# One level of Strassen's algorithm in the last big product of a three-stage kernel

## The chip, the cores and the metric

The kernel runs on one core of a Trainium2 chip. Its metric is device time in microseconds (us), from the program's start to its end, and the time given is the median of three runs. PE (TensorE) multiplies matrices, DVE (VectorE), ACT (ScalarE) and POOL (GpSimd) work element by element, SP (SyncE) issues the transfers between DRAM and the core's on-chip memory (SBUF). Matrix products land in PSUM, eight banks of 128 x 512 float32. Each engine works through its own list in order; an instruction that must wait holds up all behind it on that engine.

## The reference: attention with pooled keys, then two MoE layers

```python
k_p = k.reshape(B, H, Sp, pool, D).mean(axis=3)          # pool = 8, Sp = 72
v_p = v.reshape(B, H, Sp, pool, D).mean(axis=3)
attn = softmax(q @ k_p.T / sqrt(D)) ; x = attn @ v_p     # x: 4608 x 512

h = x @ w_in                                             # 512 x 2048
g = where(h > 0, h, exp(min(h, 0)) - 1)
x1 = g @ w_out                                           # 2048 x 512

h = x1 @ w_in2                                           # 512 x 1024
e = exp(h - max(h)) ; solu = h * e / (sum(e) + 1e-9)
ln = (solu - mean(solu)) / sqrt(var(solu) + 1e-6) * g_ln
out = ln @ w_out2                                        # 1024 x 512
```

Everything is float32 (the weights come as the two halves of float64). To keep float32 accuracy on PE, each operand is split into a high part (rounded to PE's float32r format) and a low part (the rest), and each product is made of three: high x high, low x high, high x low.

## The kernel before

The kernel has two phases. In the first, nine blocks of 512 tokens pass through the first MoE, one after the other, and the attention that makes their input runs beside them. A block has 16 slots, one for each 128 columns of w_in; a slot is 12 matmuls of 128 x 512 (`m_h1`, L420) and 12 for the slot before it (`m_o1`, L453), with the ELU between them on ACT and DVE (`m_elu`, `m_glo`: L425, L431, L432, L434, L441). The weights of w_out are split again in each slot (`w_out_split`: ACT L402, POOL L403). A block's result goes to DRAM as `x1d` (`m_out`, L466). In blocks 1 to 6 the kernel also converts the second MoE's weights to float32, splits them and stores them in DRAM (`prep`, 16 pieces, to `w2d`); `fetch` brings them back during the last block, into the buffers that the first MoE's weights leave.

The second phase takes 36 tiles of 128 tokens. `p2_load` brings 512 tokens (a chunk) of x1 back, `p2_split` splits them on ACT (L482) and DVE (L483). `p2_h2` makes h for one tile: 24 matmuls (4 slices of the inner dimension x 3 x 2 halves of the 1024 columns) into two PSUM banks, and then the softmax and the normalisation on DVE, ACT and POOL (L502 to L513). `p2_T` transposes the result on PE (8 transposes, L523) and splits it (ACT L526, DVE L527); `p2_o` is the product with w_out2, 24 matmuls (L538), whose result ACT scales (L541) and SP stores. The loop at the end runs a pipeline of three tiles: h of tile i, then the output product of tile i-2, then the transposes of tile i-1. So between the last matmul of a tile's h and its transposes lie the 24 matmuls of another tile.

The text of the kernel is not the order on each engine: outside the part marked `manual_schedule`, a scheduler with its own estimate of durations orders the instructions, and the waits are derived tile by tile from who writes and reads each tile. The PSUM pool has four banks in two buffers of tag A (two banks each, for h and for the first MoE's output) and two buffers of one bank each of tags B and C.

Of the kernel before, what the change touches and what calls it, by code (L numbers as in the profile page):

```python
# [18 lines left out]
def kernel(  # L19
# [67 lines left out]
    def att_load(i, what="kqv"):  # L87
# [115 lines left out]
    def att_T(i, h):  # L203

        es, vt = st["a", i]
        if h == 0:
            st["aT", i] = sb.tile([SK, 2, S], F32, name=f"a{i}", tag="a")
# [102 lines left out]
    w2h, w2l, o2h, o2l = {}, {}, {}, {}  # L310
# [51 lines left out]
    def prep_load(c):  # L362

        g, kk = divmod(c, 4)
        raw = sb.tile([P, 512], I64, name="raw2", tag="cv", bufs=2)
        src = w_in2[kk * P:(kk + 1) * P, g * 512:(g + 1) * 512] if c < 8 else w_out2[(c - 8) * P:(c - 7) * P, :]
        nc.sync.dma_start(out=raw, in_=src)
        wraw["p", c] = raw

    def prep(c):  # L370

        raw = wraw.pop(("p", c)).bitcast(U32)
        hw, lw = raw[:, 1::2], raw[:, 0::2]
        t = sb.tile([P, 2, 512], F32R, name="cv2", tag="cv", bufs=2)
        h, l = t[:, 0], t[:, 1]
        w = l.bitcast(F32)
        wu = l.bitcast(U32)
# [13 lines left out]
    def fetch(n):

        g, hl = divmod(n, 2)
        t = wtile("w2")
        nc.sync.dma_start(out=t.bitcast(F32), in_=w2d[:, g, hl])
        (w2h, w2l, o2h, o2l)[hl + 2 * (g // 2)][g % 2] = t
# [12 lines left out]
    o1 = {}  # L409
    gt = {}  # L410
    wo_t = {}

    def m_h1(j, f):
# [10 lines left out]
        e = sb.tile([P, 512], F32, name="e", tag="e")  # L424
# [3 lines left out]
    def m_elu(j, f):  # L428
# [4 lines left out]
        gh = sb.tile([P, 512], F32R, name="gh", tag="gh")  # L433
# [321 lines left out]
```

## Time and profile before

| | before |
|---|---|
| time, median of 3 runs | 1414.27 us (1413.56 to 1414.76) |
| the profiled execution | 1413.46 us, its span 1411.7 us |
| PE busy | 1362.0 us (96%) |
| DVE busy | 791.5 us (56%) |
| ACT busy | 588.8 us (42%) |
| POOL busy | 301.4 us (21%) |
| TensorE's granted clock, mean | 0.985 |
| start of the second phase | at 980.1 us |

The span runs from the first to the last instruction; the 1.8 us beside it are before and behind the traced instructions. Busy time of PE is time in which a matmul runs; the idle time that is left lies mostly in the first 200 us, where the attention's first units and the first weights are made. A timeline row gives the start, the duration of a merged run of instructions, the engine, line, operation, and in brackets how long the engine sat idle before it and what released it.

### The profile page before, as it was taken

The numbers are of one execution on the slowest core, as the hardware profiler recorded it, in microseconds if no ns is written. First come the engines' busy times: TensorE is split into PE (matmuls) and PEld (weight loads), VectorE is DVE, ScalarE is ACT, GpSimd is POOL, SyncE is SP. The second block draws the span as 40 slices with busy tenths as digits, with TensorE's granted clock in tenths as the row PEclk, the third lists the DMA queues.
The fourth block names the chain that finished last, engine by engine and source line by source line (L and its number), as shares of the span: only waits on it lengthen the run. The fifth ranks groups of instructions, "written<-read, shape, count | busy, mean of one in ns | idle before, by whom it ended". The sixth has DMA issues, their size and how long they took to land.

```text
span 1411.7 us, 16688 instructions
## 1 busy us (share of the span) xinstructions
PE 1362.0 (96%) x6368; PEld 1093.8 (77%) x6368; DVE 791.5 (56%) x1312; ACT 588.8 (42%) x1161; POOL 301.4 (21%) x245
## 2 busy tenths in 40 slices
PE   5788899999999999999999999999999999999998
PEld 3466677878878788788787788887888888888886
DVE  7799987886555555455554333433644554455442
ACT  3466554554444444344444333433433333333332
POOL 2345432322222322222223222221000000000000
PEclk7699999999999999999999999999999999999999
DMA  7355454461111011111010000314101110110000
GB/s 218 111 183 163 140 188 139 147 205 48 42 65 38 30 65 42 28 62 43 26 39 1 30 31 1 119 60 170 55 26 50 52 53 25 51 52 23 23 23 30
DMA packets 46991, 102.26 MB, mean 72 GB/s; under 512 B 4544, under 2 KB 12736, under 8 KB 45888
## 3 DMA queue, kind: packets, MB, share of 16 engines
q1 hardware_dynamic: 46912, 101.21, 21.5%
q8 instruction: 50, 0.82, 0.2%
q14 instruction: 29, 0.24, 0.1%
HBM read 73.93 MB, written 27.26 MB: 72 GB/s over the span
## 4 chain that ended last, share of the span: by engine, by line
PE 85%; DVE 8%; DMA 3%; ACT 2%; issue 1%; POOL 1%; SPq 0%; ACTq 0%; DVEq 0%
PE h L420 24%; PE o L453 24%; PE po L538 14%; PE h L494 14%; PE pt L523 2%; PE at L160 2%; PE at L235 2%; PE pt L211 2%; DMA raw<-in_w 1%; DMA q<-in_q 1%; DMA w2d<-cv 1%; DVE wo L343 1%; DVE wo L345 1%; DVE e L431 1%; DVE cv L345 1%
## 5 line engine op out<-in xcount | busy, mean ns | idle before, releaser
L403 POOL TENSOR_TENSOR wol<-wo,woh 128x512 fp32r<-128x512 f32 x144 | 206.6, 1435 | 541.0 <-ACT woh L402 541.0
L420 PE MATMUL h<-xh,wh 128*128 128x512 f32 x576 | 236.7, 411 | 0.8 <-ACT xh L248 0.4
L453 PE MATMUL o<-gh,woh 128*128 128x512 f32 x576 | 228.2, 396 | 6.6 <-ACT gh L434 3.4
L453 PE MATMUL o<-gh,wol 128*128 128x512 f32 x576 | 227.4, 395 | 0.8 <-POOL wol L403 0.8
L420 PE MATMUL h<-xl,wh 128*128 128x512 f32 x576 | 227.6, 395 | 0.0
L420 PE MATMUL h<-xh,wl 128*128 128x512 f32 x576 | 226.4, 393 | 0.7 <-POOL wl L360 0.7
L538 PE MATMUL po<-w,dhl 128*128 128x512 f32 x864 | 202.7, 390 | 1.8 <-ACT dhl L526 1.8
L431 DVE TENSOR_SCALAR e<-e 128x512 f32<-128x512 f32 x144 | 65.4, 454 | 242.1 <-ACT e L425 242.0
L538 PEld LDWEIGHTS po<-w,dhl 128*128 128x128 f32 x864 | 161.9, 188 | 36.5 <-ACT dhl L526 2.3
L494 PE MATMUL h<-w,x1h 128*128 128x512 f32 x576 | 186.5, 395 | 0.3 <-DVE x1s L465 0.3
L425 ACT ACTIVATE e<-h 128x512 f32<-128x512 f32 x144 | 85.9, 597 | 216.4 <-PE h L420 216.2
L434 ACT CAST gh<-e 128x512 fp32r<-128x512 f32 x144 | 89.5, 621 | 155.0 <-DVE e L432 155.0
L420 PEld LDWEIGHTS h<-xh,wh 128*128 128x128 f32 x576 | 108.9, 189 | 34.9 <-issue 13.6
L453 PEld LDWEIGHTS o<-gh,woh 128*128 128x128 f32 x576 | 108.8, 189 | 32.6 <-ACT gh L434 5.6
L453 PEld LDWEIGHTS o<-gh,wol 128*128 128x128 f32 x576 | 108.9, 189 | 24.9 <-POOL wol L403 1.3
L420 PEld LDWEIGHTS h<-xl,wh 128*128 128x128 f32 x576 | 108.7, 189 | 25.1 <-DVE xl L249 0.4
L420 PEld LDWEIGHTS h<-xh,wl 128*128 128x128 f32 x576 | 109.1, 189 | 22.0 <-POOL wl L360 1.4
L494 PEld LDWEIGHTS h<-w,x1h 128*128 128x128 f32 x576 | 108.2, 188 | 22.3 <-DVE x1s L465 0.7
L494 PE MATMUL h<-w,x1l 128*128 128x512 f32 x288 | 112.3, 390 | 0.0
L503 ACT ACTIVATE e<-h,sc 128x1024 f32<-128x1024 f32 x36 | 40.2, 1117 | 165.4 <-DVE sc L502 165.1
L513 POOL TENSOR_TENSOR sc<-sc,mhalf 128x1 f32<-128x1 f32 x36 | 19.7, 548 | 400.7 <-DVE sc L512 400.7
L402 ACT CAST woh<-wo 128x512 fp32r<-128x512 f32 x144 | 89.3, 621 | 35.4 <-PE o L453 31.0
(524 smaller groups left out, 1873.6 us busy)
## 6 DMA issues: line engine op xcount, KB each, us to landing
raw<-in_w SPq DMA_DIRECT2D x53, 512.0 KB
v<-in_v SPq DMA_DIRECT2D x32, 288.0 KB
x1d<-x1s SPq DMA_DIRECT2D x9, 1024.0 KB
x1r<-x1d SPq DMA_DIRECT2D x9, 1024.0 KB
out<-ot SPq DMA_DIRECT2D x36, 256.0 KB
w2d<-cv SPq DMA_DIRECT2D x16, 512.0 KB
w<-w2d SPq DMA_DIRECT2D x8, 1024.0 KB
k<-in_k SPq DMA_DIRECT2D x28, 288.0 KB
```

The costliest lines, as they stand in the source:

```text
L160: nc.tensor.matmul(s[:, t * 2 * SK:(t + 1) * 2 * SK], q_t[:, o:o + P], kp, start=True, stop=True)
L211: nc.tensor.transpose(pt[0:SK, t * P:(t + 1) * P], es[:, 2 * t + h, :], ident)
L402: nc.scalar.copy(oh, t[:, f % 4, :])
L403: nc.gpsimd.tensor_tensor(ol, t[:, f % 4, :], oh.bitcast(F32), op=ALU.subtract)
L420: nc.tensor.matmul(h[:, 0:n], a[g][:, kk, fo:fo + P], x[j][:, kk, 0:n], start=(i == 0), stop=(i == 3 * KDM - 1))
L425: nc.scalar.activation(e[:, 0:n], h[:, 0:n], AF.Exp)
L431: nc.vector.tensor_scalar(e[:, 0:n], e[:, 0:n], 1.0, 1.0, op0=ALU.min, op1=ALU.subtract)
L434: nc.scalar.copy(gh[:, 0:n], e[:, 0:n])
L453: nc.tensor.matmul(acc, a[:, dm * P:(dm + 1) * P], x[:, 0:n], start=(f == 0 and m == 0), stop=(f == NF - 1 and m == 2))
L494: nc.tensor.matmul(h[:, g, :], a[c][:, kk, o:o + P], w[g][:, kk, :], start=(m == 0), stop=(m == 3 * KDM - 1))
L503: nc.scalar.activation(e, hv, AF.Exp, bias=sc[:, 0:1], accum_out=sc[:, 1:2])
L538: nc.tensor.matmul(po, a[:, c, :], w[c // 4][:, c % 4, :], start=(m == 0), stop=(m == 3 * NC2 - 1))
```

## The change

The product x1 @ w_in2 is made by one level of Strassen's algorithm in Winograd's form. Two tiles of 128 tokens form a pair (rows 1 and 2 of A), the inner dimension of 512 is cut in two halves of 256, and w_in2 is cut in four quarters of 256 x 512 (B11, B12, B21, B22). Instead of eight products of quarters there are seven, `prod`, each of 6 matmuls (2 slices x 3): A11 B11, A12 B21, S1 T1, S2 T2, S3 T3, A22 T4, S4 B22, where S1 to S4 are sums of quarters of A and T1 to T4 of quarters of B. Bank X gathers A11 B11, S2 T2, S3 T3 and A22 T4 in this order, Y holds A12 B21, Z gathers S1 T1 and S4 B22. Between the products, `snap` copies X to SBUF on ACT three times (sn), because three of the four results need X as it stands at that moment; DVE adds the copies to Y and Z (L572, L575, L583) and ACT copies the finished X (L581). The results, ha and hb for the two tiles, lie in SBUF, where before h was read from PSUM.

- `p2_split` makes S1 to S4 for a pair (four sums of 128 x 256, L524 to L527) and splits 1792 columns for a pair (L530, L531, L533, L534), where before it split 1024.
- The matrices for w_in2 are made by `prep_in` in the last two blocks of the first MoE: conversion, then four differences, then seven splits, stored in `w2d`; the eight pieces of w_out2 are made in blocks 1 to 4 and stored in `o2d`. `fetch` loads eleven matrices of 1 MB in the last block (before: eight), four of w_out2 and seven for w_in2; three of these (T1, T2, T4) go to buffers of w_out.
- The pools of tiles used in one phase only are p1 and p2, and p2 takes the place of p1.
- The loop at the end goes over 18 pairs: five products of pair n (`p2_h_one`), the transposes of the first tile of pair n-1, the output product of the second tile of pair n-2, two products (`p2_h_two`) and the softmax of both tiles (`p2_soft`), the split of the next pair, the output product of the first tile of pair n-1 and the transposes of its second tile.

```diff
-    w2d = dr.tile([P, 4, 2, 4, 512], F32, name="w2d")
+    w2d = dr.tile([P, 7, 4, 512], F32, name="w2d")
+    o2d = dr.tile([P, 2, 2, 4, 512], F32, name="o2d")
...
+    W2 = {"B11": 0, "T1": 1, "T2": 2, "B21": 3, "T3": 4, "T4": 5, "B22": 6}
+    def prep_in(a, step):
+        if step < 4:
+            if step == 0:
+                st["F"], st["G"] = xtile("F", F32), xtile("G", F32)
+            prep_conv(8 + 4 * (step % 2) + 2 * (step // 2) + a, st["F"][:, step])
+            return
+        F, G = st["F"], st["G"]
+        ...
+        if step == 4:
+            for o, x, y in ((t1, b12, b11), (t3, b22, b12), (t2, b22, t1), (t4, b21, t2)):
+                nc.vector.tensor_tensor(o, x, y, op=ALU.subtract)
+        ...
+            nc.scalar.copy(t[:, 0], w)
+            nc.vector.tensor_tensor(t[:, 1], w, t[:, 0].bitcast(F32), op=ALU.subtract)
+            nc.sync.dma_start(
+                out=w2d[:, W2[n]].rearrange("p (h a) f -> p h a f", a=2)[:, :, a], in_=t.bitcast(F32)
...
-    def p2_split(c):
-        t = wraw.pop(("x", c))
-        x1h[c], x1l[c] = xtile(f"x1h{c}"), xtile(f"x1l{c}")
-        for kk in range(KDM):
-            nc.scalar.copy(x1h[c][:, kk, :], t[:, kk, :])
-            nc.vector.tensor_tensor(x1l[c][:, kk, :], t[:, kk, :], x1h[c][:, kk, :].bitcast(F32), op=ALU.subtract)
+    def p2_split(n):
+        c, q = divmod(n, 2)
+        t = wraw["x", c]
+        ta, tb = slice(q * P, (q + 1) * P), slice(256 + q * P, 256 + (q + 1) * P)
+        sm = sb.tile([P, 4, 2, P], F32, name=f"xs{n}", tag="cv", bufs=2)
+        hi, lo = (xtile(f"x{k}{n}").rearrange("p a f -> p (a f)") for k in "hl")
+        tt = nc.vector.tensor_tensor
+        tt(sm[:, 0], t[:, 0:2, tb], t[:, 2:4, tb], op=ALU.add)
+        tt(sm[:, 1], sm[:, 0], t[:, 0:2, ta], op=ALU.subtract)
+        tt(sm[:, 2], t[:, 0:2, ta], t[:, 0:2, tb], op=ALU.subtract)
+        tt(sm[:, 3], t[:, 2:4, ta], sm[:, 1], op=ALU.subtract)
+        for src, d in ((t[:, :, ta], slice(0, 512)), (t[:, 2:4, tb], slice(512, 768))):
+            h, l = (z[:, d].rearrange("p (k t) -> p k t", t=P) for z in (hi, lo))
+            nc.scalar.copy(h, src)
+            tt(l, src, h.bitcast(F32), op=ALU.subtract)
+        src = sm.rearrange("p s k t -> p (s k t)")
+        nc.scalar.copy(hi[:, 768:1792], src)
+        tt(lo[:, 768:1792], src, hi[:, 768:1792].bitcast(F32), op=ALU.subtract)
...
+    def prod(n, bank, a, b, start, stop):
+        hi, lo = xc[n]
+        w = w2[b]
+        m = 0
+        for k in range(2):
+            o = (2 * A[a] + k) * P
+            for x, y in ((hi, 0), (lo, 0), (hi, 2)):
+                nc.tensor.matmul(
+                    bank, x[:, o:o + P], w[:, y + k, :], start=(start and m == 0), stop=(stop and m == 5),
+                    skip_group_check=True,
+                )
+                m += 1
+    def snap(bank):
+        t = p2.tile([P, 512], F32, name="sn", tag="sn", bufs=3)
+        nc.scalar.copy(t, bank)
+        return t
+    def p2_h_one(n):
+        xy = ps.tile([P, 2, 512], F32, name="xy", tag="A")
+        z = ps.tile([P, 2, 512], F32, name="z", tag="A")
+        X, Y, Z = xy[:, 0], xy[:, 1], z[:, 0]
+        ha = p2.tile([P, 2, 512], F32, name="ha", tag="h", bufs=3)
+        hb = p2.tile([P, 2, 512], F32, name="hb", tag="h", bufs=3)
+        prod(n, X, "A11", "B11", True, False)
+        p1s = snap(X)
+        prod(n, Z, "S1", "T1", True, False)
+        prod(n, X, "S2", "T2", False, False)
+        u2s = snap(X)
+        prod(n, Y, "A12", "B21", True, True)
+        nc.vector.tensor_tensor(ha[:, 0], Y, p1s, op=ALU.add)
+        prod(n, X, "S3", "T3", False, False)
+        u3s = snap(X)
+        nc.vector.tensor_tensor(hb[:, 1], Z, u3s, op=ALU.add)
+        acc[n] = (X, Z, ha, hb, u2s)
+    def p2_h_two(n):
+        X, Z, ha, hb, u2s = acc.pop(n)
+        prod(n, X, "A22", "T4", False, True)
+        nc.scalar.copy(hb[:, 0], X)
+        prod(n, Z, "S4", "B22", False, True)
+        nc.vector.tensor_tensor(ha[:, 1], Z, u2s, op=ALU.add)
+        xc.pop(n)
+        c, q = divmod(n, 2)
+        p2_soft(4 * c + q, ha)
+        p2_soft(4 * c + q + 2, hb)
...
-        nc.scalar.activation(sq, e, AF.Square, accum_out=sc[:, 3:4])
+        nc.scalar.activation(hv, e, AF.Square, accum_out=sc[:, 3:4])
...
-        if 1 <= j <= 6 and f % 5 == 0 and 3 * (j - 1) + f // 5 < 16:
-            prep_load(3 * (j - 1) + f // 5)
-        if 1 <= j <= 6 and f % 5 == 2 and 3 * (j - 1) + f // 5 < 16:
-            prep(3 * (j - 1) + f // 5)
+        if 1 <= j <= 4 and f in (1, 8):
+            with tc.issue_after(gate[j - 1] if f == 1 else gate["ld"]):
+                prep_load(2 * (j - 1) + f // 8)
+        if 1 <= j <= 4 and f in (3, 10):
+            prep(2 * (j - 1) + f // 8)
+        n = (j - NBLK + 2) * NF + f
+        a, n = divmod(n, 11)
+        if 0 <= a < 2:
+            if 1 <= n <= 4:
+                with tc.issue_after(gate[NBLK - 3]):
+                    prep_load(8 + 4 * ((n - 1) % 2) + 2 * ((n - 1) // 2) + a)
+            if 2 <= n <= 10:
+                prep_in(a, n - 2)
         if j == NBLK - 1 and f % 4 == 3:
-            fetch(f // 2 - 1)
-            fetch(f // 2)
+            for n in (("B11", "T1", "B21"), ("T2", "T3", "B22"), ("T4", (0, 0), (0, 1)), ((1, 0), (1, 1)))[f // 4]:
...
-    for i in range(NTILE + 2):
-        if i < NTILE:
-            p2_h2(i)
-        if i % 4 == 1:
-            c = i // 4 + 1
-            if c * 512 < NT:
-                p2_split(c)
-            if (c + 1) * 512 < NT:
-                p2_load(c + 1)
-        if 2 <= i:
-            p2_o(i - 2)
-        if 1 <= i <= NTILE:
-            p2_T(i - 1)
+    first.close()
+    p2 = ctx.enter_context(tc.tile_pool(name="p2", bufs=2, reuse_waits="tile"))
+    def tiles_of(n):
+        c, q = divmod(n, 2)
+        return 4 * c + q, 4 * c + q + 2
+    for n in range(NPAIR + 2):
+        if n < NPAIR:
+            p2_h_one(n)
+        if 1 <= n <= NPAIR:
+            p2_T(tiles_of(n - 1)[0])
+        if n < NPAIR and n % 2 == 0 and n // 2 + 1 < NT // 512:
+            p2_load(n // 2 + 1)
+        if n >= 2:
+            p2_o(tiles_of(n - 2)[1])
+        if n < NPAIR:
+            p2_h_two(n)
+        if n + 1 < NPAIR:
+            p2_split(n + 1)
+        if 1 <= n <= NPAIR:
+            p2_o(tiles_of(n - 1)[0])
+            p2_T(tiles_of(n - 1)[1])
```

The rows below are the order of three engines in the second phase, of before and after, with the semaphores that an instruction waits for; the numbers in names tell buffers apart. First ACT's list around one tile of before (e_9346, L511 is the Square of the normalisation, L526 the splits behind the transposes) and around one pair after (e_9280 and e_9292 are its two tiles):

```order
L503 ACTIVATE e_9346,sc<-h_9320,sc 128x1024 [waits DVE_49,Activation_49]
...
L541 ACTIVATE ot<-po,sc 128x512 [waits DMAHW5_49,PE_49,Pool_49]
L511 ACTIVATE e_9346,sc<-e_9346 128x1024 [waits DVE_49]
L526 CAST dhl<-pt_9386 128x512 [waits PE_49]
L526 CAST dhl<-pt_9393 128x512 [waits PE_49]
```

```order
L596 ACTIVATE e_9280,sc<-ha,sc 128x1024 [waits DVE_49]
L596 ACTIVATE e_9292,sc<-hb,sc 128x1024 [waits DVE_49]
L635 ACTIVATE ot<-po,sc 128x512 [waits DMAHW5_49,PE_49,Pool_49]
L620 CAST dhl<-pt_9345 128x512 [waits PE_49]
L620 CAST dhl<-pt_9352 128x512 [waits PE_49]
L557 COPY sn<-xy 128x512 [waits PE_49]
L605 ACTIVATE ha,sc<-e_9280 128x1024 [waits DVE_49,Activation_49]
L557 COPY sn<-xy 128x512 [waits PE_49]
L605 ACTIVATE hb,sc<-e_9292 128x1024 [waits DVE_49,Activation_49]
L620 CAST dhl<-pt_9402 128x512 [waits PE_49]
L620 CAST dhl<-pt_9409 128x512 [waits PE_49]
L557 COPY sn<-xy 128x512 [waits DVE_49,PE_49]
```

The three copies of X (L557) stand between the normalisation's steps of the pair before; the second copy stands behind the Square of ha, which waits for DVE.

DVE's list of before from a tile's maximum to the end of its softmax, and after from the last sum of a pair (L583) to the end of its first tile's softmax (L603):

```order
L502 TENSOR_REDUCE sc<-h_9148 128x1 [waits PE_49,Pool_49]
L504 TENSOR_SCALAR sc<-sc 128x1 [waits Activation_49]
L505 RECIPROCAL sc<-sc 128x1 [waits DVE_49]
L506 SCALAR_TENSOR_TENSOR e_9174,sc<-e_9174,sc,h_9148 128x1024 [waits DVE_49]
L509 TENSOR_SCALAR sc<-sc 128x1 [waits DVE_49]
L510 TENSOR_SCALAR e_9174<-e_9174,sc 128x1024 [waits DVE_49]
```

```order
L583 TENSOR_TENSOR ha<-z,sn 128x512 [waits PE_49]
L531 TENSOR_TENSOR xl_9484<-x1r_9235,xh_9483 128x256
L595 TENSOR_REDUCE sc<-ha 128x1 [waits DVE_49,Pool_49]
L595 TENSOR_REDUCE sc<-hb 128x1 [waits Activation_49,Pool_49]
L534 TENSOR_TENSOR xl_9484<-xs_9482,xh_9483 128x1024
L597 TENSOR_SCALAR sc<-sc 128x1 [waits Activation_49]
L524 TENSOR_TENSOR xs_9842<-x1r_9595 128x256 [waits DMAHW7_49,DVE_49]
...
L599 SCALAR_TENSOR_TENSOR e_9280,sc<-e_9280,sc,ha 128x1024 [waits DVE_49]
L598 RECIPROCAL sc<-sc 128x1 [waits DVE_49]
L621 TENSOR_TENSOR dhl<-pt_9345,dhl 128x512 [waits Activation_49]
...
L599 SCALAR_TENSOR_TENSOR e_9292,sc<-e_9292,sc,hb 128x1024 [waits DVE_49]
L603 TENSOR_SCALAR e_9280<-e_9280,sc 128x1024 [waits DVE_49]
```

The second tile's steps and the next pairs' splits and sums now stand between the steps of the first tile.

PE's list of after around the same place, each product shown by its first row (T_7509 is T2, B_7345 is B21, T_7511 is T3, T_7663 is T4, B_7513 is B22), behind two rows of before, where the transposes are followed by the next tile's h:

```order
L523 MATMUL pt_9466<-ident,e_9346 128x128 [waits PE_49]
...
L523 MATMUL pt_9473<-ident,e_9346 128x128 [waits PE_49]
...
L494 MATMUL h_9480<-w_7323,x1h_9185 128x512
L494 MATMUL h_9480<-w_7323,x1l_9186 128x512
L494 MATMUL h_9480<-w_7325,x1h_9185 128x512
```

```order
L549 MATMUL xy<-T_7509,xh_9304 128x512 [waits Activation_49]
...
L617 MATMUL pt_9402<-ident,e_9280 128x128 [waits DVE_49,PE_49]
...
L617 MATMUL pt_9409<-ident,e_9280 128x128 [waits DVE_49]
...
L549 MATMUL xy<-B_7345,xh_9304 128x512 [waits Activation_49]
...
L632 MATMUL po<-o_7665,dhl 128x512
L632 MATMUL po<-o_7667,dhl 128x512
L632 MATMUL po<-o_7665,dhl 128x512 x2
L549 MATMUL xy<-T_7511,xh_9304 128x512 [waits DVE_49]
...
L549 MATMUL xy<-T_7663,xh_9304 128x512 [waits Activation_49]
...
L549 MATMUL z<-B_7513,xh_9304 128x512 [waits DVE_49]
```

Every product now waits for ACT or DVE. B21 writes bank Y, but X and Y are one tile (xy), so it waits for the second copy of X; T3 waits for L572, which reads Y. Between T2 and B21 stand eight transposes, between B21 and T3 four matmuls, between T3 and T4 twenty.

## Rows read from the trace of the kernel before

**Rows 1.** The page: the span, and each engine's busy time, share and instructions.

```profile
span 1411.7 us, 16688 instructions
PE 1362.0 (96%) x6368; PEld 1093.8 (77%) x6368; DVE 791.5 (56%) x1312; ACT 588.8 (42%) x1161; POOL 301.4 (21%) x245
```

**Rows 2.** Busy time by stretch: PE, PEld, DVE, ACT, POOL, clock, DMA share, GB/s.

```profile
800.00:900.00 100.00, 100.00 (x438) 81.48 (x435) 35.69 (x60) 35.63 (x61) 23.25 (x18) 1.00 0.09 31
1150.00:1200.00 50.00, 50.00 (x239) 41.71 (x238) 25.16 (x47) 17.84 (x33) 2.19 (x4) 1.00 0.13 44
```

**Rows 3.** PE's timeline in the second phase, from one output product to the next.

```profile
997.55 5.61 PE L538 MATMUL po<-w,dhl 128*128 128x512 f32 x24
1003.00 1.03 PE L523 MATMUL pt<-ident,e 128*128 128x128 f32 x8
...
1009.32 5.61 PE L538 MATMUL po<-w,dhl 128*128 128x512 f32 x24
```

**Rows 4.** Groups by line and shape, mean ns of one, DVE and ACT.

```profile
L527 DVE TENSOR_TENSOR dhl<-pt,dhl 128x512 fp32r<-128x512 f32 x72 | 46.5, 686 | 32.6 <-ACT dhl L526 32.6
L506 DVE SCALAR_TENSOR_TENSOR e<-e,sc,h 128x1024 f32<-128x1024 f32 x36 | 46.1, 1281 | 1.5
L510 DVE TENSOR_SCALAR e<-e,sc 128x1024 f32<-128x1024 f32 x36 | 27.1, 754 | 1.2
L483 DVE TENSOR_TENSOR x1l<-x1r,x1h 128x512 fp32r<-128x512 f32 x32 | 20.6, 685 | 19.1 <-PE h L494 19.1
L249 DVE TENSOR_TENSOR xl<-at,xh 128x256 fp32r<-128x256 f32 x8 | 3.4, 420 | 2.1 <-ACT xh L248 2.1
L526 ACT CAST dhl<-pt 128x512 fp32r<-128x512 f32 x72 | 38.2, 586 | 0.0
```

**Rows 5.** Timeline of all engines around two tiles of the second phase.

```profile
1198.10 0.52 SPq L475 DMA_DIRECT2D x1r<-x1d  x1
1198.49 1.22 DVE L502 TENSOR_REDUCE sc<-h 128x1 f32<-128x1024 f32 x1
1199.63 1.89 DVE L483 TENSOR_TENSOR x1l<-x1r,x1h 128x512 fp32r<-128x512 f32 x3
1201.43 0.14 DVE L504 TENSOR_SCALAR sc<-sc 128x1 f32<-128x1 f32 x1
...
1203.43 1.14 ACT L482 CAST x1h<-x1r 128x512 fp32r<-128x512 f32 x2 [2.42 <-DMA x1r<-x1d]
...
1205.06 1.05 ACT L511 ACTIVATE e<-e 128x1024 f32<-128x1024 f32 x1
...
1206.10 1.06 ACT L526 CAST dhl<-pt 128x512 fp32r<-128x512 f32 x2
...
1209.71 5.61 PE L538 MATMUL po<-w,dhl 128*128 128x512 f32 x24
1209.98 1.22 DVE L502 TENSOR_REDUCE sc<-h 128x1 f32<-128x1024 f32 x1 [1.98 <-PE h L494]
```

**Rows 6.** Timeline at the end: PE waits for a split, then the last scaling.

```profile
1393.65 1.06 ACT L526 CAST dhl<-pt 128x512 fp32r<-128x512 f32 x2
1394.28 6.01 PE L538 MATMUL po<-w,dhl 128*128 128x512 f32 x24 [1.29 <-ACT dhl L526]
...
1407.86 0.69 ACT L541 ACTIVATE ot<-po,sc 128x512 f32<-128x512 f32 x1 [5.75 <-PE po L538]
```

**Rows 7.** The chain that ended last, where the second phase begins.

```profile
980.08 11.18 PE h L494 x48
```

**Rows 8.** PE's busy time and granted clock in two stretches with pauses.

```profile
100.00:104.00 4.00, 1.82 (x8) 1.00 0.24 52
104.00:108.00 4.00, 2.76 (x14) 1.00 0.73 283
228.00:232.00 4.00, 2.34 (x10) 1.00 0.37 111
232.00:236.00 4.00, 4.00 (x14) 0.57 0.40 156
```

More of the change, by code (lines that the diff above doesn't have):

```diff
@@ L206, in att_T @@
         if h == 0:
[L207 removed]
+            st["aT", i] = p1.tile([SK, 2, S], F32, name=f"a{i}", tag="a")
         a = st["aT", i]
@@ L362, in prep_load, with prep_conv @@
     def prep_load(c):
-        g, kk = divmod(c, 4)
         raw = sb.tile([P, 512], I64, name="raw2", tag="cv", bufs=2)
-        src = w_in2[kk * P:(kk + 1) * P, g * 512:(g + 1) * 512] if c < 8 else w_out2[(c - 8) * P:(c - 7) * P, :]
-        nc.sync.dma_start(out=raw, in_=src)
+        if c < 8:
+            nc.sync.dma_start(out=raw, in_=w_out2[c * P:(c + 1) * P, :])
+        else:
+            g, kk = divmod(c - 8, 4)
+            nc.sync.dma_start(out=raw, in_=w_in2[kk * P:(kk + 1) * P, g * 512:(g + 1) * 512])
         wraw["p", c] = raw
-    def prep(c):
+    def prep_conv(c, w):
         raw = wraw.pop(("p", c)).bitcast(U32)
         hw, lw = raw[:, 1::2], raw[:, 0::2]
[L374 to L377, printed above, removed]
+        wu = w.bitcast(U32)
         nc.scalar.activation(w, hw.bitcast(F32), AF.Abs, scale=2.0**-112)
@@ L391, in fetch, with prep @@
[L391 to L396, printed above, removed]
+    def prep(c):
+        t = sb.tile([P, 2, 512], F32R, name="cv2", tag="cv", bufs=2)
+        h, l = t[:, 0], t[:, 1]
+        w = l.bitcast(F32)
+        prep_conv(c, w)
+        gs = gl[:, c:c + 1]
+        nc.scalar.activation(h, w, AF.Copy, scale=gs)
+        nc.vector.scalar_tensor_tensor(l, w, gs, h.bitcast(F32), op0=ALU.mult, op1=ALU.subtract)
+        nc.sync.dma_start(out=o2d[:, c // 4, :, c % 4], in_=t.bitcast(F32))
@@ new lines @@
+    W2 = {"B11": 0, "T1": 1, "T2": 2, "B21": 3, "T3": 4, "T4": 5, "B22": 6}
[6 more added lines that the diff above has]
+        F, G = st["F"], st["G"]
+        b11, b12, b21, b22 = (F[:, i] for i in range(4))
+        t1, t2, t3, t4 = (G[:, i] for i in range(4))
+        if step == 4:
+            for o, x, y in ((t1, b12, b11), (t3, b22, b12), (t2, b22, t1), (t4, b21, t2)):
+                nc.vector.tensor_tensor(o, x, y, op=ALU.subtract)
+            return
+        for n, w in (
+            (("B11", b11), ("T1", t1)), (("T2", t2), ("B21", b21)), (("T3", t3), ("T4", t4)), (("B22", b22),)
+        )[step - 5]:
+            t = sb.tile([P, 2, 512], F32R, name="cv2", tag="cv", bufs=2)
+            nc.scalar.copy(t[:, 0], w)
[3 more added lines that the diff above has]
+            )
@@ L401, in w_out_split @@
-        ol = sb.tile([P, 512], F32R, name="wol", tag="wol")
+        oh = p1.tile([P, 512], F32R, name="woh", tag="woh")
+        ol = p1.tile([P, 512], F32R, name="wol", tag="wol")
         nc.scalar.copy(oh, t[:, f % 4, :])
@@ L476, in p2_load @@
         wraw["x", c] = t
[L478 to L497 removed]
+    def p2_split(n):
[16 more added lines that the diff above has]
+        tt(lo[:, 768:1792], src, hi[:, 768:1792].bitcast(F32), op=ALU.subtract)
+        xc[n] = (hi, lo)
+        if q == 1:
+            wraw.pop(("x", c))
```

86 lines of the change are left out of this document (40 added, 46 removed).

## The prediction

> **What bounds the kernel now.** I read the page first: PE is busy for 1362.0 us of a span of 1411.7 us, DVE for 56% and ACT for 42% of it [rows 1]. The busy times by stretch say where: in the last blocks of the first MoE and in the second phase PE works in every microsecond (100.00 of 100, 50.00 of 50), and DVE fills 25 of 50 us, ACT 18 [rows 2]. So a removed matmul saves its time only as long as nothing makes PE wait; what DVE and ACT do costs nothing until PE waits for it. PE's timeline gives the prices: 24 matmuls take 5.45 us (997.55 to 1003.00), 0.227 us each, and from one output product to the next, 48 matmuls and 8 transposes, it is 11.77 us, so 8 transposes cost 0.87 us [rows 3]. Two tiles take 23.54 us. The second phase begins at 980.1 us [rows 7], and the last scaling on ACT begins at 1407.86 [rows 6]: 427.8 us, of which 36 x 11.77 = 423.7 are PE's work.
>
> **What is removed.** h takes 18 x 42 = 756 matmuls in place of 864. 108 x 0.227 = 24.5 us less; PE's work in the second phase is 399.2 us, 22.18 per pair. If nothing waited, that would be the gain.
>
> **What is added on the path.** In a pair PE has seven products, each waiting for ACT or DVE. The order shows the ring that counts: B21 waits for the second copy of X; on ACT this stands behind the Square of the pair before, which waits for DVE's L603, which ends the softmax of that pair's first tile; and that softmax starts with L583, after the last product (B22) of that pair. So from one B22 to the next there is one chain, whatever PE has to do. I walk it with prices from rows, the clock at 0 where PE goes on after B22. Prices: PE to DVE 0.27 (1209.71 to 1209.98), a maximum of 1024 columns 1.14 to the next instruction, three 512-wide differences 1.89 together, so 0.60 from one to the next, Square to the next ACT instruction 1.04 [rows 5]; a split on ACT 0.59, and PE 0.04 behind it (1393.65 + 0.586 to 1394.28) [rows 4, 6]. A difference of 1024 columns is not in the trace: from 256 and 512 columns (420 and 685 ns) I estimate 1.21, 1.13 to the next [rows 4]; the product with accumulation (L506, 1.28) I take at 1.30 to the next instruction, small ones at 0.1 to 0.2.
>
> - DVE: L583 starts at 0.27, the 512-wide split 0.88, the two maxima 1.52 and 2.66, the 256-wide split 3.81, L597 4.15, the 1024-wide split 4.27, three small steps and a sum 5.40, the product for the first tile 5.95, a split behind transposes (L621) 7.36, the product for the second tile 8.08, L603 9.38, done at 10.13. ACT's two exponentials (from 2.84 and 3.94) are done before DVE asks for them.
> - ACT: Square 10.17, copy of X 11.21, done 11.80. PE waits from about 11.15 and starts B21 at 11.84.
> - B21 takes 1.36 and 0.14 for the cold start (my share of 6.01 against 5.61 us for 24 matmuls with two waits [rows 3, 6]). L572 reads Y at 13.61 and is done 14.35 (0.69 and the hand-over); T3 15.85; 21 output matmuls 20.6; T4 and B22 23.33.
>
> That is for every second pair. In the others the loaded chunk x1r (issued at the end of B22; from issue to use 1198.10 to 1203.43, 5.33 us [rows 5]) lets L524 start only at 5.55, and four sums stand in the chain: L603 ends at 10.63, the interval is 23.60. The mean is 23.47, 1.29 above PE's work; 16 intervals make 20.6 us. All other work (split of the next pair, output products, transposes) lies inside the intervals. Bounds for an interval: 22.2 if the waits go, 24.2 if every DVE step costs its whole duration with a hand-over (I add 0.05 to 0.1 to each of a dozen steps).
>
> Start: the first pair has no output products between its products. B21, T3 and T4 each wait about 1 us for a copy or for L572; in the second pair B21 waits 1.7 and the first transposes 2.9, since the softmax of the first pair is the only work behind them, and T4 and B22 1.7 more with their cold starts. By the same walk the second B22 ends 28.8 us after the start, with 20.8 of PE's work: 8.0. The first product may start 0.5 earlier, as one of the two accumulators is done before the other. Tail: four output products, with the splits behind Square on ACT: 3.7 of waiting. Second phase: 399.2 + 20.6 + 8.0 - 0.5 + 3.7 + 0.3 (PE to the last scaling) = 431.3, against 427.8: **+3.5 us**.
>
> The first phase: conversion and differences for w_in2 put up to 4 us of DVE work between two ELUs in a slot of 5.5 us in blocks 7 and 8, where DVE is busy for 36% [rows 2]; I estimate one or two waits of PE, 1.5 us together (bounds 0 and 5). The prep that leaves blocks 1 to 6 gives nothing, PE being full there. The fetches (eleven in place of eight) end before their product asks, except perhaps x1r1, which has 6.5 us until L572.
>
> [...]
>
> Sum: 1413.46 + 3.5 + 1.5 + 2.9 = 1421.4 for an execution like the profiled one, which is 0.8 below the median: **1422 us**, 0.55% slower.
>
> [...]
>
> **Rivals.**
> - *The waits are hidden and PE bounds it* (the other side: faster). Place: B21's wait. DVE and ACT are half idle now [rows 2]; if L603 ended at 8.9 and not at 10.1 to 10.6, no wait would be left in the intervals: 1422 - 20.6 - 2.9 = 1399. Against it: DVE has 10 us of work in its list ahead of L603, and only the order could shorten that. It decides from an interval of 22.8 on, where the sum falls to 1411. Chance 0.14, with all that ends under 1411.4.
> - *Break-even*: intervals of 22.9 to 23.2, since some steps overlap more than in before: 1411.4 to 1417. Chance 0.18.
> - *The forecast*, intervals of 23.2 to 23.9: 1417 to 1430. Chance 0.50.
> - *Longer steps or a falling clock*: whole durations (+0.7 per interval, 12 us), or the clock falls in each pair: 17 x 1.7 = 29, so 1430 to 1448. For it: the waits of a pair (T2, the transposes, B21, T3) lie close together, as at 228 us. Against it: most clusters in the trace left the clock alone. Chance 0.18. [...]
>
> **How the numbers follow.** The likeliest case gives 1422. The range leaves 0.1 at either end: 1411 to 1438. A measurement of this kernel tells 0.2% from no change, 1411.4 to 1417.1: faster 0.14, the same 0.18, slower 0.68.
>
> **What would show it.** Right: the profile after has PE waiting for sn (L557), e (L603) and ha (L572) in each pair, about 1.3 us per pair beyond its work; a pair takes 23.3 to 23.6 us; DVE is busy for over 70% in the second phase; the second phase lasts about 431 us; the first ends within 3 us of 980. Wrong: a pair takes 22.2 us and PE shows no waits, or granted clocks of 0.5 appear in the second phase, or PE waits in blocks 7 and 8 for more than 5 us.

## The result: faster, not slower

| | before | after |
|---|---|---|
| time, median | 1414.51 us (1413.11 to 1418.2, 6 runs) | 1401.96 us (1399.86 to 1404.09, 6 runs) |
| ratio after / before | | 0.9907, 95% interval 0.9888 to 0.9925 |
| profiled execution, its span | 1413.46, 1411.7 us | 1404.09, 1402.3 us |
| first product of the second phase | 980.08 | 976.09 |
| second phase, to the start of the last scaling | 427.8 us | 422.7 us |

The change gains 12.5 us, 0.9%. I had forecast 1422 us, a loss of 0.55%, and the result lies below my range (1411 to 1438). On the page after, against [rows 1], PE has 108 matmuls fewer, and DVE and ACT are busier by 72 and 60 us.

```profile
span 1402.3 us, 16772 instructions
PE 1344.3 (96%) x6260; PEld 1070.7 (76%) x6260; DVE 863.5 (62%) x1470; ACT 649.1 (46%) x1257; POOL 302.9 (22%) x245
```

In the same two stretches as in [rows 2] PE is no longer full, by 0.94 and 0.39 us, and DVE fills 33 of 50 us in the second phase (I had said over 70%).

```profile
800.00:900.00 100.00, 99.06 (x427) 79.60 (x427) 60.95 (x98) 44.85 (x77) 25.80 (x18) 1.00 0.36 127
1150.00:1200.00 50.00, 49.61 (x233) 40.12 (x232) 32.73 (x71) 27.10 (x49) 3.08 (x5) 1.00 0.12 43
```

**The first phase, before and after.** I had read that PE is full in blocks 1 to 6 and that the prep there costs nothing. Windows of the kernel before that lie ahead of those in [rows 2] say otherwise. The first begins at a marker in block 0, the 65th output matmul of the first phase, which every kernel here has (at 106.34). The columns are those of [rows 2]:

```profile
106.00:190.00 84.00, 75.78 (x353) 57.21 (x354) 80.14 (x101) 49.39 (x122) 37.97 (x22) 1.00 0.47 155
190.00:300.00 110.00, 106.83 (x507) 84.11 (x506) 85.51 (x139) 55.44 (x109) 31.13 (x21) 0.98 0.50 166
```

After, where the marker comes at 109.12:

```profile
109.00:190.00 81.00, 74.92 (x355) 57.76 (x355) 72.56 (x89) 47.25 (x118) 37.17 (x22) 1.00 0.39 125
190.00:300.00 110.00, 110.00 (x534) 88.47 (x533) 69.05 (x116) 49.49 (x98) 29.70 (x21) 1.00 0.24 74
```

Before, DVE was busy for 80 of 84 us at the end of block 0, and PE lost 8.2 us there and 3.2 behind it, where its clock was also lower (0.98 in the mean). After, PE loses 6.1 at the end of block 0 and nothing behind it. Part of DVE's work there is the prep, and SP's timeline of before shows when it ran (start, duration, line; raw is a piece of weights loaded, w2d a piece stored, x1d a block's result):

```profile
146.91 0.43 SPq L367 DMA_DIRECT2D raw<-in_w  x1
...
167.89 0.38 SPq L389 DMA_DIRECT2D w2d<-cv  x1
...
189.49 0.63 SPq L466 DMA_DIRECT2D x1d<-x1s  x1
...
325.91 0.39 SPq L389 DMA_DIRECT2D w2d<-cv  x1
```

The sixteen pieces, which the text of the kernel spreads over blocks 1 to 6 (the last behind 706 us), were pulled forward by the scheduler: the first is loaded 43 us before block 0 is stored, the last is stored at 325.9. After, each load is held behind the store of the block before or a load of the attention:

```profile
186.44 0.62 SPq L501 DMA_DIRECT2D x1d<-x1s  x1
187.16 0.57 SPq L369 DMA_DIRECT2D raw<-in_w  x1
...
217.88 0.42 SPq L369 DMA_DIRECT2D raw<-in_w  x1
...
288.77 0.54 SPq L501 DMA_DIRECT2D x1d<-x1s  x1
289.36 0.62 SPq L369 DMA_DIRECT2D raw<-in_w  x1
```

From the marker to the second phase it was 873.7 us (106.34 to 980.08), now it is 867.0 (109.12 to 976.09): 6.8 less, in spite of 2.2 us more behind the seventh block's store (172.5 to 174.7), where the new prep for w_in2 stands (no run tests that prep by itself). A second profile of the changed kernel (e11) has 867.2 and 174.9.

**A pair.** This is PE's timeline of one pair, from the end of B22 to the end of the next, against [rows 3] (xy<-B at 1152.74 is B21, xy<-T at 1155.20 is T3; the end of a product is taken where PE goes on behind it):

```profile
1141.35 5.67 PE L632 MATMUL po<-o,dhl 128*128 128x512 f32 x24
1146.86 1.04 PE L617 MATMUL pt<-ident,e 128*128 128x128 f32 x8
1147.65 0.48 PE L549 MATMUL xy<-B,xh 128*128 128x512 f32 x1
...
1151.84 0.82 PE L617 MATMUL pt<-ident,e 128*128 128x128 f32 x6
1152.74 0.50 PE L549 MATMUL xy<-B,xh 128*128 128x512 f32 x1
...
1154.39 0.95 PE L632 MATMUL po<-o,dhl 128*128 128x512 f32 x3
1155.20 0.50 PE L549 MATMUL xy<-T,xh 128*128 128x512 f32 x1
...
1164.24 5.67 PE L632 MATMUL po<-o,dhl 128*128 128x512 f32 x24
```

This pair takes 22.89 us and the next (to 1187.27) 23.03; the sixteen intervals behind the second B22 (1004.31 to 1370.41) have a mean of 22.88, where bare work is 22.18 and I had 23.47. DVE's chain in this pair, with its prices (answering to [rows 4, 5]):

```profile
1141.55 0.69 DVE L583 TENSOR_TENSOR ha<-z,sn 128x512 f32<-128x512 f32 x1 [6.00 <-PE z L549]
...
1142.76 1.21 DVE L595 TENSOR_REDUCE sc<-ha 128x1 f32<-128x1024 f32 x1
1143.89 1.21 DVE L595 TENSOR_REDUCE sc<-hb 128x1 f32<-128x1024 f32 x1
...
1147.00 1.28 DVE L599 SCALAR_TENSOR_TENSOR e<-e,sc,ha 128x1024 f32<-128x1024 f32 x1
...
1149.01 1.28 DVE L599 SCALAR_TENSOR_TENSOR e<-e,sc,hb 128x1024 f32<-128x1024 f32 x1
...
1150.21 0.75 DVE L603 TENSOR_SCALAR e<-e,sc 128x1024 f32<-128x1024 f32 x1
```

and what ACT does behind it:

```profile
1151.06 1.07 ACT L605 ACTIVATE ha<-e 128x1024 f32<-128x1024 f32 x1 [0.82 <-DVE sc L602]
...
1152.12 0.57 ACT L557 COPY sn<-xy 128x512 f32<-128x512 f32 x1
```

The order is the one I walked. L603 ends 9.61 us behind B22, not 10.13, and B21 starts at 11.39, not 11.84; from there to the next B22 it is 11.50, as walked (11.49). In the second kind of pair, every other one, where DVE waits for a newly loaded chunk, L603 ends 10.01 behind B22, not 10.63, and B21 starts at 11.79, 0.50 after its eight transposes would be through (0.79, as from 1146.86 to 1147.65 above; in the first kind six transposes stand ahead of B21):

```profile
1169.58 0.43 DVE L524 TENSOR_TENSOR xs<-x1r 128x256 f32<-128x256 f32 x1 [0.29 <-DMA x1r<-x1d]
...
1174.74 1.04 PE L617 MATMUL pt<-ident,e 128*128 128x128 f32 x8
1176.03 0.50 PE L549 MATMUL xy<-B,xh 128*128 128x512 f32 x1 [0.25 <-ACT sn L557]
```

How long these pairs wait differs between executions. DVE waits 0.27 to 0.32 us for the chunk here, and B21 then 0.25 to 0.30 for its copy; in e11, the same kernel, B21 waits 0.37 to 0.40, and pairs of the second kind take 23.0 to 23.1 here and 23.2 to 23.4 there; those of the first kind take about 22.87 in both, but for one of 23.2.

The second B22 ends 28.2 us after the start (walked: 28.8, less 0.5), and the last scaling starts 28.35 behind the last of the sixteen intervals (my sum had 431.3 - 28.3 - 375.5 = 27.5 for it). PE's granted clock is 1.00 throughout the second phase.

### The profile page after: what moved, and what is told of

Same layout as the page of the kernel before. It is cut to its first block, busy times and chain, and to the rows that moved or that the text cites. A ratio compares the mean times of both kernels' runs of the same rounds, so it can differ in the third digit from the quotient of the medians.

```text
span 1402.3 us, 16772 instructions
## 1 busy us (share of the span) xinstructions
PE 1344.3 (96%) x6260; PEld 1070.7 (76%) x6260; DVE 863.5 (62%) x1470; ACT 649.1 (46%) x1257; POOL 302.9 (22%) x245
## 3 DMA queue, kind: packets, MB, share of 16 engines
q1 hardware_dynamic: 48256, 104.88, 22.5%
## 4 chain that ended last, share of the span: by engine, by line
PE 75%; DVE 14%; DMA 5%; ACT 3%; issue 2%; POOL 0%; SPq 0%; DVEq 0%; ACTq 0%
PE o L488 24%; PE h L455 24%; PE po L632 9%; PE xy L549 7%; DVE e L599 2%; PE z L549 2%; PE at L163 2%; DMA x1r<-x1d 2%; PE at L238 2%; PE pt L214 2%; DVE sc L595 1%; DMA k<-in_k 1%; ACT ha L605 1%; DMA raw<-in_w 1%; PE pt L617 1%
## 5 line engine op out<-in xcount | busy, mean ns | idle before, releaser
L632 PE MATMUL po<-o,dhl 128*128 128x512 f32 x864 | 209.4, 394 | 2.0 <-ACT dhl L620 2.0
L632 PEld LDWEIGHTS po<-o,dhl 128*128 128x128 f32 x864 | 161.3, 188 | 37.3 <-ACT dhl L620 2.5
L467 DVE TENSOR_TENSOR e<-e,h 128x512 f32<-128x512 f32 x144 | 98.9, 687 | 3.7
L549 PE MATMUL xy<-T,xh 128*128 128x512 f32 x216 | 78.0, 402 | 1.6 <-DVE ha L572 0.9
L635 ACT ACTIVATE ot<-po,sc 128x512 f32<-128x512 f32 x36 | 24.7, 687 | 86.1 <-PE po L632 79.0
L204 POOL TENSOR_TENSOR es<-es,sm 128x720 f32<-128x720 f32 x28 | 41.2, 1472 | 100.5 <-DVE sm L202 92.4
```

The source lines that it names most:

```text
L204: eng.tensor_tensor(es, es, bc(sm, NG), op=ALU.mult)
L467: nc.vector.tensor_tensor(e[:, 0:n], e[:, 0:n], h[:, 0:n], op=ALU.max)
L549: nc.tensor.matmul(bank, x[:, o:o + P], w[:, y + k, :], start=(start and m == 0), stop=(stop and m == 5), skip_group_check=True,)
L632: nc.tensor.matmul(po, a[:, c, :], w[c // 4][:, c % 4, :], start=(m == 0), stop=(m == 3 * NC2 - 1))
```

## Experiments

The table gives medians beside the kernel before on the same chip (1414.29 us for e1 to e4, 1414.95 for e5 to e8, 1413.10 for e9 to e11). The interval is the mean of the sixteen behind the second B22; it, the start (to the second B22) and the tail come from PE's timeline as above.

| kernel | us | ratio to before (95%) | interval | start | tail |
|---|---|---|---|---|---|
| the change, again (e11) | 1401.61 | 0.9921 (0.9907 to 0.9936) | 22.97 | 28.2 | 28.3 |
| e1 Y in z | 1389.43 | 0.9842 (0.9814 to 0.9871) | 22.51 | 24.5 | 28.3 |
| e2 longer chain | 1393.66 | 0.9859 (0.9842 to 0.9875) | 22.49 | 28.4 | 28.2 |
| e3 both | 1387.28 | 0.9818 (0.9804 to 0.9833) | 22.34 | 24.3 | 28.2 |
| e4 old prep rhythm | 1409.78 | 0.9972 (0.9960 to 0.9984) | 22.94 | 28.2 | 28.3 |
| e5 Square behind the copy | 1398.02 | 0.9885 (0.9868 to 0.9902) | 22.75 | 29.7 | 27.2 |
| e6 two more passes | 1398.25 | 0.9889 (0.9873 to 0.9906) | 22.65 | 29.6 | 28.6 |
| e7 before, with the gate | 1405.32 | 0.9939 (0.9918 to 0.9960) | | | |
| e8 e5 and e1 | 1385.69 | 0.9807 (0.9784 to 0.9831) | 22.32 | 23.9 | 27.2 |
| e9 transposes ahead | 1403.41 | 0.9925 (0.9908 to 0.9941) | 22.73 | 33.2 | 29.9 |
| e10 e5 and e9 | 1396.87 | 0.9887 (0.9870 to 0.9904) | 22.43 | 32.6 | 27.2 |

In e9 and e10 the first of the sixteen intervals is only 20.7 us, because the pair ahead of it is so long (in the others it is 21.8 to 22.6). Without the first, the means are 22.87 in e9, 22.55 in e10 and 23.05 in e11. By steady pairs I mean all but the first two and the last three.

**The prep: e4 and e7.** e4 gives the changed kernel the old rhythm for w_out2's pieces:

```diff
-        if 1 <= j <= 4 and f in (1, 8):
-            with tc.issue_after(gate[j - 1] if f == 1 else gate["ld"]):
-                prep_load(2 * (j - 1) + f // 8)
+        if 1 <= j <= 3 and f % 5 == 0 and 3 * (j - 1) + f // 5 < 8:
+            prep_load(3 * (j - 1) + f // 5)
...
```

> The changed kernel with the eight pieces of w_out2 in the rhythm of before: three to a block from block 1 on, their loads not held back. Theory rhythm (the first phase is shorter after the change because the third piece in a block made the ELU late, PE waiting for gh and gl for 3.2 us between 182 and 320 us): these waits come back, 1404 to 1406 us, and the first phase ends about 3 us later. Rival (the 4 us are the differences that any two executions have in the first 200 us): 1401 to 1403 us, no waits for gh and gl behind 190 us.

It costs 8 us, more than either theory had. The first load goes back to 146.64, and blocks 0 and 1 lose 6.7 of the 10.1 us that they had gained (marker to the second block's store: 189.7 us before, 179.7 in the changed kernel, 186.4 here). To the second phase it is 873.1 us, 6.2 more than in the changed kernel; the second phase itself is unchanged. e7 gives the kernel before the new rhythm and the gate, for all sixteen pieces, with no Strassen:

```diff
-        if 1 <= j <= 6 and f % 5 == 0 and 3 * (j - 1) + f // 5 < 16:
-            prep_load(3 * (j - 1) + f // 5)
+        if 1 <= j <= 7 and f in (1, 8):
+            with tc.issue_after(gate[j - 1] if f == 1 else gate["ld"]):
+                prep_load(2 * (j - 1) + f // 8)
...
```

> The kernel before, without Strassen, with its sixteen pieces of the second MoE's weights two to a block in blocks 1 to 6 and four in block 7, their loads held behind the store of the block before or a load of the attention, as the changed kernel does it. Theory prep (in the kernel before all sixteen pieces ran between 147 and 296 us, ahead of their blocks, on a full DVE, and PE waited for the ELU): PE's waits behind 106 us go, the first phase is about 9 us shorter, 1404 to 1408 us. Rival (the difference of the first phases was mostly the start, which varies by 6 us between executions): 1410 to 1415 us.

It gains 9.6 us (by the interval of the ratio, 6 to 12), as theory prep said (the last piece was stored at 326, not 296 as I wrote there). From the marker to the second block's store it takes 179.75 us, as the changed kernel does, and to the second phase 866.2, 7.6 less than before. The window that lost PE's 3.2 us is full:

```profile
190.00:300.00 110.00, 110.00 (x532) 88.36 (x531) 69.19 (x113) 49.37 (x98) 31.21 (x22) 1.00 0.21 64
```

So most of the change's gain is not Strassen's: 9.6 of 12.5 us by the medians, and by the rows behind the marker 7.6 of 11.9 (6.8 in the first phase and 5.1 in the second). e7 changes the rhythm and the gate together; which of the two does it was not tested. Between e7 and the changed kernel lie 3.4 to 3.7 us by the medians (2.5 to 4.5 by the ratios to before), near what the second phase gives (5.1) less the new prep (2.2).

**What sets a pair: e1 to e3.** e1 is one line:

```diff
-        X, Y, Z = xy[:, 0], xy[:, 1], z[:, 0]
+        X, Y, Z = xy[:, 0], z[:, 1], z[:, 0]
```

> The changed kernel with Y (A12 B21) in the free second bank of tile z instead of the second bank of xy, so that B21 does not wait for the second copy of X, nor T3 for the sum that reads Y. Theory ring (the interval of a pair is set by the chain from B22 through DVE, Square and the second copy of X to B21, 22.88 us in the profile after): the chain no longer holds B21, T3 needs the copy only 1.4 us later; 0.25 us of wait and 0.3 us of cold starts per pair go, intervals of 22.2 to 22.5, and 2 to 3 us at the start; 1389 to 1395 us. Rival (the 0.7 us above the 22.18 of bare work is PE's own, in switches between products and transposes; only the 0.1 us listed as waits goes): 1399 to 1402 us.

The time is as the ring had it and the interval just above, but the scheduler also moved T3 to stand right behind B21 and the transposes behind T3, so this alone does not tell the ring from any other wait on the tile xy. e2 adds a maximum on DVE, e3 is e2 with e1's line:

```diff
+        if i % 4 < 2:
+            nc.vector.tensor_reduce(sc[:, 5:6], hv, axis=AX, op=ALU.max)
         nc.vector.tensor_scalar(e, e, sc[:, 2:3], None, op0=ALU.subtract)
```

> The changed kernel with one more maximum over 1024 columns (1.13 us on DVE, its result unused) ahead of the subtraction that ends the softmax of a pair's first tile. Theory ring: each of 16 intervals grows by the whole 1.13, and the first pairs and the tail by about 1 to 2 us; intervals of 24.0, 1419 to 1422 us. Rival (PE bounds the pair and the chain is only just in time, DVE being busy for two thirds): the maximum is mostly hidden, 1402 to 1408 us.

> Both edits: Y in z's second bank, and the extra maximum of 1.13 us ahead of the subtraction. Theory ring: with B21 free, T3 is the first product to need the second copy of X, about 1.4 us after B21 could start, so the extra 1.13 us is nearly hidden: 0 to 4 us above the kernel with Y in z alone, 16 to 25 us below the kernel with the extra maximum alone. Rival (the work on DVE itself sets the pace, whatever B21 waits for): as far above the kernel with Y in z alone as the extra maximum costs without it.

Both theories failed in e2: with more work it is 8 us faster than the changed kernel. The scheduler had drawn other lists: all eight transposes and an output matmul ahead of B21, five to seven ahead of T3, and the subtraction L603 (here L605) ahead of the second tile's product. An edit that adds an instruction was no test of a duration here. It did show that DVE's amount of work is not what bounds a pair, and e3 that 22.34 can be had with it.

**The ring by itself: e5 and e6.** e5 issues the Square behind the second copy of X of the next pair (`behind`), its unused output in a tile of its own. In the steady pairs PE's products and all but the small steps on DVE keep their order, but the transposes do not: six of them stand ahead of B21 in every pair, where the changed kernel has eight in pairs of the second kind.

```diff
+            with tc.issue_after(behind):
+                nc.scalar.activation(jk, e, AF.Square, accum_out=sc[:, 3:4])
```

> The changed kernel with the Square of both tiles (and the two small steps behind it) issued behind the second copy of X of the next pair; the Square's unused output goes to a bf16 tile of its own. In the steady pairs DVE's list keeps its order, PE's products stand as in the changed kernel, and on ACT the copy of X now stands ahead of the Square. Theory ring (PE waits because that copy stood behind the Square): 0.25 us of wait and its cold start go, the wait of T3 for the sum that reads Y stays; intervals 22.4 to 22.6 us in place of 22.88, 1393 to 1398 us. Rival (PE's own switches make the 0.7 us above bare work, or DVE sets the pace): intervals of 22.8 to 22.9, 1400 to 1404 us.

The steady intervals are 22.8, as the rival said, and not 22.5; the time, 1398.0, is below the rival's 1400 to 1404, with a tail that is 1.1 us shorter. PE's and ACT's timelines show why, and it is not PE's switches. PE:

```profile
1146.69 0.82 PE L627 MATMUL pt<-ident,e 128*128 128x128 f32 x6
1147.53 0.50 PE L549 MATMUL xy<-B,xh 128*128 128x512 f32 x1
...
1169.50 0.85 PE L627 MATMUL pt<-ident,e 128*128 128x128 f32 x6
1170.34 0.50 PE L549 MATMUL xy<-B,xh 128*128 128x512 f32 x1
```

ACT:

```profile
1146.89 0.59 ACT L557 COPY sn<-xy 128x512 f32<-128x512 f32 x1 [1.85 <-PE xy L549]
1147.37 1.06 ACT L615 ACTIVATE jk<-e 128x1024 bf16<-128x1024 f32 x1
```

The copy, now ahead of the Square, starts 0.20 after T2 ends (1146.69), takes 0.59, and B21 starts 0.05 later: 0.84, of which six transposes cover about 0.6 (six eighths of 0.79). Behind the ring lay a second, nearly equal wait of the same instruction. In pairs of the first kind the ring was worth only some 0.04 us (22.87 to 22.83); in those of the second kind the two transposes that now stand behind B21 (0.2 us) take back part of what the cut ring gave. e6 makes the softmax longer by two passes over e, and the scheduler then sets the copy ahead of the Square itself:

```diff
+        if i % 4 < 2:
+            for _ in range(2):
+                nc.vector.tensor_scalar(e, e, 1.0, None, op0=ALU.mult)
         nc.vector.tensor_scalar(e, e, sc[:, 2:3], None, op0=ALU.subtract)
```

> The changed kernel with two more passes over e (1024 columns times 1.0, about 0.66 us each on DVE) ahead of the subtraction that ends the softmax of a pair's first tile. The scheduler answers by setting the second copy of X ahead of the Square, and four output matmuls ahead of B21. Theory ring: the copy no longer stands behind the softmax, so more work on DVE makes the pair shorter than in the changed kernel: intervals 22.3 to 22.6, 1393 to 1398 us. Rival (the work on DVE ahead of the subtraction sets the pace, 1.3 us longer): intervals of 23.5 to 24.2, 1412 to 1424 us.

The interval is 22.65, just above what the ring had. So DVE's pace is out, but the ring is not the whole: in every second pair T3 waits up to 0.25 us for the sum that reads Y (L572).

**Both waits: e9 and e10.** The new theory (account A) is that B21 waits for its copy of X, which starts behind the Square or behind T2, whichever is later, and that PE idles for what the matmuls between T2 and B21 do not cover. e9 makes PE take all eight transposes of the pair before (`mid`) ahead of B21; in that list up to nine output matmuls stand ahead of T3. e10 adds e5's edit.

```diff
-        prod(n, Y, "A12", "B21", True, True)
+        mid()
+        with tc.issue_after(gate["pt"]) if "pt" in gate else ExitStack():
+            prod(n, Y, "A12", "B21", True, True)
```

> The changed kernel with all eight transposes ahead of B21 in every pair (before: six in every second one) and nine output matmuls ahead of T3 where there were three; ACT and DVE keep their order. Account A (both waits count: in pairs with the 1792-column split on ACT the copy of X starts when T2 ends, 0.84 us before B21 can start, and only 0.65 us of transposes stand ahead; in the others the softmax and the Square make the copy late by 0.42 us): the first kind falls from 22.9 to 22.5, the second stays at 23.0, mean 22.75, 1399 to 1402 us. Account B (the ring through the softmax alone): both kinds stay, mean 22.88. Account C (the copy behind T2 alone): both kinds fall to 22.5, 1394 to 1398 us.

> Both edits of order: the Square behind the second copy of X, and eight transposes ahead of B21, with six output matmuls ahead of T3. Account A: no wait is left in a steady pair, intervals 22.4 to 22.55 us, 1392 to 1396 us. Accounts B and C would give what one of the edits alone gives, and the rival of the runs before (PE's own switches) 22.8.

> The changed kernel again, unedited, beside the two edits of order: 1400 to 1404 us, pairs of 22.85 to 22.95 us; the first block's store anywhere between 180 and 187 us, since that is where executions differ.

In e9 two neighbouring pairs, the first kind and then the second, look like this:

```profile
1150.62 1.04 PE L619 MATMUL pt<-ident,e 128*128 128x128 f32 x8
1151.50 0.50 PE L549 MATMUL xy<-B,xh 128*128 128x512 f32 x1
...
1173.10 1.20 PE L619 MATMUL pt<-ident,e 128*128 128x128 f32 x8
1174.70 0.50 PE L549 MATMUL xy<-B,xh 128*128 128x512 f32 x1 [0.40 <-ACT sn L557]
```

and in e10 like this:

```profile
1152.55 1.03 PE L629 MATMUL pt<-ident,e 128*128 128x128 f32 x8
1153.38 0.50 PE L549 MATMUL xy<-B,xh 128*128 128x512 f32 x1
...
1175.18 1.23 PE L629 MATMUL pt<-ident,e 128*128 128x128 f32 x8
1176.16 0.47 PE L549 MATMUL xy<-B,xh 128*128 128x512 f32 x1
```

The steady intervals of e9 alternate between 22.46 to 22.50 (first kind) and 23.2 to 23.4 (second kind); the changed kernel beside it (e11) has about 22.87 and 23.2 to 23.4. So the first kind fell and the second stayed, as account A has it. That the mean of 22.73 hits account A's 22.75 is luck, since the short first interval is in it. e10's are 22.5 to 22.6 throughout. So each edit takes one of the two waits, and only both take them all; what e10 still has above e8's 22.3 was not tested. Neither order is free: in the second pair the transposes now hold up B21 until the only softmax is done, and the start goes from 28.2 to 33 us. e9 as a whole is 1.8 us slower than the changed kernel beside it, which is within the spread of the runs; its second phase lasts 426.8 us and that of e11 424.1.

**e8**, e5 with e1's line, has the lowest median here (the intervals of its ratio and of e3's overlap):

> The Square behind the second copy of X, and Y in z's second bank. Theory ring: Y in z frees T3 from the sum that reads Y and B21 from the copy; the late Square then adds little: intervals 22.2 to 22.45 us (22.51 with Y in z alone), the first two pairs as with Y in z (24.5 us to the second B22), 1384 to 1389 us. Rival (the late Square delays the scaling of the output products or the splits behind it on ACT): 1390 to 1396 us.

B21, now in z's bank, needs no copy; T3, behind it, needs T2's copy, 0.84 us, and B21's six matmuls take 1.36. Nothing is left to wait for in a steady pair:

```profile
1141.88 1.04 PE L627 MATMUL pt<-ident,e 128*128 128x128 f32 x8
1142.67 5.75 PE L642 MATMUL po<-o,dhl 128*128 128x512 f32 x24
1148.26 0.40 PE L549 MATMUL xy<-T,xh 128*128 128x512 f32 x1
```

Its 22.32 is within 0.15 of bare work. It is 29 us under the kernel before, and the new rhythm with its gate alone is worth 9.6 of them (e7).

## Why the prediction was wrong

Against the profiled execution (predicted 1421.4, measured 1404.09, 17.3 less), by its steps:

- *"The prep that leaves blocks 1 to 6 gives nothing, PE being full there"*: this step failed. I took from the text where the prep runs, and the order on SP has it elsewhere, at the end of block 0 and in block 1, where PE was not full. First phase: +1.5 predicted, -6.8 measured from the marker on, 8.3 off. Its other half was near: 1.5 for blocks 7 and 8, 2.2 measured. e4 and e7 show it: the old rhythm alone costs 6.2 us of the first phase, the new one alone gives 7.6.
- *The interval of 23.47*: 0.59 too long, 9.4 us over sixteen. The chain and its order were right, the prices of the steps on DVE were not: from L583 to L603's end 9.4 us and not 9.86. The largest part, 0.18, is the product, two times 1.21 to the next instruction and not 1.30; the small steps took 0.06 and not 0.1 to 0.2, so that an error of some hundredths stood in a dozen steps. The break-even rival had such intervals (22.9 to 23.2), and I chose the longer ones. That the ring alone sets the interval was wrong as well: with the ring cut (e5) 22.8 remain, and with both waits taken (e10) 22.55.
- *The clock*, 2.9 us of the sum: an estimate of mine, a tenth of 17 x 1.7, where 1.7 us is what a granted clock of 0.57 costs in the four us from 232 us on [rows 8]. No run shows the term: in the second phase of the changed kernel the granted clock is 1.00, in the mean and in each window of four us, and the clock cost nothing. That *most clusters in the trace left the clock alone* holds only from 72 us on (between there and 300 us the windows of four us show one fall, that at 232); ahead of that the kernel before ran at 0.50 in several stretches (20 to 24, 28 to 44 and 52 to 56 us).
- *Start and tail*: 28.3 and 27.5 predicted, 28.2 and 28.35 measured; right within 0.9.
- *The start of the program* (not in the sum): the marker came 2.8 us later in this execution. In the thirteen profiles it lies between 103.2 and 109.1, whatever the edit; the two profiles of the changed kernel are 4.1 us apart in it, and what causes that stays open.

8.3 + 9.4 + 2.9 + 0.1 - 0.85 - 2.8 = 17.05 of the 17.3. *108 matmuls fewer* was right, and so was that waits of PE take back most of it: 24.5 us are removed and 5.1 are left. The time itself lies where I had put the rival of hidden waits (under 1411.4, chance 0.14), but not by its mechanism: B21 still waits in a pair, and the first phase, which that rival left alone, gave more than half of the gain.

That maxima and products read h from SBUF after the change, and before from PSUM, is not what made the chain short: a maximum of 1024 columns takes 1.21 us from SBUF here, and 1.22 from PSUM in [rows 5]; a difference of 512 columns takes 685 ns with both operands in SBUF and 686 with one in PSUM [rows 4]. A clock that falls in each pair, as the last rival had it, is not seen in any of the seventeen pairs of the changed kernel, where the granted clock is 1.00.

## What to carry to other kernels

Where a scheduler sets the order, read from the issue times where a moved step really ran before you price its removal; the program's text is no evidence. When a wait has two causes of nearly the same length, taking one away shows only the other; look at both releasers' times before you promise the gain. And an experiment that adds work can redraw the lists: compare the lists first, and test with an edit of order or of tiles where a duration cannot be changed alone.

## What was not expected of the hardware

In the second pair of the changed kernel PE paused for 1.31 us and soon after for 2.10 us, and its clock stayed at 1.00 (the four us of each pause; PE, PEld, DVE, ACT, POOL, clock, DMA share, GB/s):

```profile
992.00:996.00 4.00, 2.69 (x12) 1.65 (x10) 4.00 (x11) 2.40 (x5) 0.00 (x0) 1.00 0.41 160
996.00:1000.00 4.00, 1.90 (x13) 1.60 (x13) 4.00 (x11) 1.74 (x4) 0.32 (x1) 1.00 0.00 2
```

In e9 one pause of 5.08 us (until 993.55) was followed by granted clocks of 0.58 and 0.57 in the windows from 992 to 1000; in those from 1000 to 1080 it was 1.00 again, and near the end, from 1376 to 1384, 0.79 and 0.78:

```profile
988.00:992.00 4.00, 0.47 (x3) 0.05 (x1) 4.00 (x12) 1.73 (x5) 0.00 (x0) 1.00 0.29 111
992.00:996.00 4.00, 2.45 (x10) 2.35 (x11) 3.77 (x11) 2.41 (x5) 0.67 (x1) 0.58 0.01 2
996.00:1000.00 4.00, 4.00 (x12) 3.12 (x12) 1.98 (x3) 0.76 (x2) 0.55 (x1) 0.57 0.00 0
```
